# Issuing TensorE in a written order, with outer products over four row quadrants at once, in an attention and MLP backward kernel

## The chip, the cores and the metric

The kernel runs on one core of one Trainium2 chip. The metric is the device time of one execution in microseconds (us). A "round" runs both kernels on the same chip, one after the other; I quote medians. On one core a run is called slow when it is more than 1.5% above the fastest run of the same kernel in the same batch, and fast otherwise. Each run lists its mean granted TensorE clock as a share of full speed.

The parts of the core, in the profile's short names: PE is TensorE (PEld its weight loads), DVE is VectorE, ACT is ScalarE, POOL is GpSimd, SP is SyncE, which issues the loads here. POOL issues the stores. SBUF is the memory on the core, PSUM the small memory that TensorE writes to.

## The reference, cut to what matters

One decode step (one query token, batch 2) of grouped-query attention with a cache plus a bilinear MLP, and the gradients of everything for a given `grad_out`:

```python
q = (layernorm(x) @ wq)                     # 32 query heads, 16 kv heads, Dh = 128
scores = einsum("bhqd,bhkd->bhqk", q, k) * Dh ** -0.5      # 4096 positions
o = einsum("bhqk,bhkd->bhqd", softmax(scores), v)
out = x + o @ wo + ((xn @ w_gate) * (xn @ w_up)) @ w_down  # F = 4608, D = 576
_out, _vjp = jax.vjp(f, A_x, A_k_cache, A_v_cache, A_wq, A_wo, B_w_gate, B_w_up, B_w_down)
```

All inputs are read once and every gradient has the size of its input: 92.5 MB in, 92.5 MB out. With one token, the gradients of the caches and of the weights are outer products. So there is little arithmetic for each byte, but it comes as many small matmuls.

## The kernel before

The main loop has 16 steps. A step takes two K heads and two V heads of one batch entry, 1 MB each. Three kinds of TensorE work fill a step:

- **Scores.** VectorE transposes half a head, then 16 matmuls of 128 columns accumulate into one PSUM tile. The 16 come as two quarters of 8.
- **Outer products** for the gradients of K and V. 128 rows are used as four quadrants of 32, each with its own matmul (`32*128` in the profile below: 32 rows, 128 weight columns). One unit of work below does two quadrants, fills one `ps_o` buffer, and is copied out ("evicted") by ACT, or sometimes DVE, into a store tile.
- **Contractions**: 64 matmuls of 32 weight columns that reduce two heads over their positions.

```python
sb  # SBUF, by tag:  "nat" 12 buffers (loads), "st" 4 (cache-gradient stores),
    #                "sw" 2 (weight-gradient stores), "X" 3 (transposed halves)
ps  # PSUM, by tag:  "m" 2, "sc" 2 (scores), "o" 2 of [P, 2, 512] FP32
def ps_o():
    return ps.tile([P, 2, 512], FP32, tag="o", bufs=2, name="ps_o")
...
def head_scores(n, t, x, s_ps, half):
    X = xtile([P, NCH, 64], "X")
    t32(view(pairs(X...)), view(pairs(n...)))           # DVE transpose, 1.23 us
    for e in range(2):
        for c8 in range(8):
            nc.tensor.matmul(s_ps[:], lhsT=view(W[t][:], ...), rhs=view(X[:], ...), ...)
...
def outer_units(rows, bd, b, l0, oview):
    def unit(A, cp):                       # A: which pair of quadrants
        def f():
            if cp == 0:
                m["st"] = stile([P, 2, 2, 8, Dh], "so")
            o = ps_o()
            for k in range(2):
                for aa in range(2):
                    a = 2 * A + aa
                    nc.tensor.matmul(view(o[:], ...), lhsT=rows[32 * a:32 * a + 32, 2 * cp + k, :],
                                     rhs=bd[32 * a:32 * a + 32, :], start=True, stop=True)
            evac(view(m["st"][:], ...), o[:]..., 1024)
            if cp == 3:                    # two stores of 512 KB
                for aa in range(2):
                    nc.gpsimd.dma_start(oview[b, 2 * A + aa, :, l0:l0 + 2], m["st"][:, aa]...)
    return [unit(A, cp) for A in range(2) for cp in range(4)]
...
def slot(src, t, b, l, s_ps, per, mid=None):
    n = head_load(src, b, l)
    head_scores(n, t, l % 2, s_ps, 0)
    more(2)                                # two outer units
    if mid: mid()
    head_scores(n, t, l % 2, s_ps, 1)
    more(2)
    other(per)                             # MLP and group work
```

Four steps share a group of heads. At a group's end its weight gradients are staged in the two "sw" buffers: `sto` (gradient of the output weight, two tiles), then `stq` (gradient of the query weight, two tiles). The MLP's staging tiles `stw` and `std` use the same two buffers.

The order of the instructions on each engine isn't the order of this text: a scheduler reorders them when the kernel is built. Each engine then works through its own list and waits for what other engines or transfers must have done.

## Time and profile before

| | before |
|---|---|
| median time (first three runs) | 571.89 us (568.31 to 573.84) |
| span of the profiled run | 561.8 us |
| PE busy, granted clock | 472.1 us (84%), 0.802 |
| ACT, DVE busy | 343.6 us (61%), 369.6 us (66%) |
| DMA engines busy | about 87% of the span |

The prediction below shows the busy shares, the slices and six windows. What it doesn't show are the four largest TensorE groups of the page. A line gives the source line, engine, operation, output and inputs, the count; after the bar the busy time in us and the mean ns of one; after the second bar the engine's idle time just before these instructions and what ended most of it.

```profile
L503 PE MATMUL ps_sc<-X,W 128*128 128x128 bf16 x2048 | 185.8, 240 | 2.5 <-DVE X L102 2.4
...
L549 PE MATMUL ps_o<-bd,prm 32*128 32x256 bf16 x512 | 52.9, 304 | 10.5 <-ACT stq L93 4.7
L549 PE MATMUL ps_o<-bd,dsm 32*128 32x256 bf16 x512 | 54.8, 302 | 6.8 <-ACT so L93 4.4
L518 PE MATMUL ps_m<-kv,rowT 128*32 128x128 bf16 x2048 | 56.3, 251 | 1.0 <-issue 0.9
```

### The profile page before, as it was taken

The page shows a single profiled execution, that of the slowest core. Times are in us where ns is not written, and L with a number is a line of the kernel's source. Part 1 is how long each engine was busy: PE and PEld are TensorE (multiplying, and loading weights), DVE is VectorE, ACT ScalarE, POOL GpSimd, SP SyncE. Part 2 cuts the span into 40 slices and gives each one's busy share as a digit, 9 for nine tenths or more (in the row PEclk, how much of TensorE's full clock was granted, in tenths as well). Part 3 has the DMA queues.
Part 4 walks back from the last instruction along what each step waited for, and adds up shares of the span by engine and source line. Part 5 has one row for each costly group of instructions (what it writes and reads, how often), then busy time and mean ns, then how long its engine had stood idle before and what let it go on. Part 6 is the DMA issues. An engine that isn't in the chain of part 4 may idle for free. (4 is left out here: it accounts for less than half of the span.)

```text
span 561.8 us, 18035 instructions
## 1 busy us (share of the span) xinstructions
PE 472.1 (84%) x7897; PEld 336.5 (60%) x7897; DVE 369.6 (66%) x637; ACT 343.6 (61%) x473; POOL 193.3 (34%) x404
## 2 busy tenths in 40 slices
PE   2688859998989799999888973999898999888842
PEld 1576637676766465676677752666676666666511
DVE  8696836747656545738577672685787567788336
ACT  1146856857666264657667662686767559778631
POOL 5222443422432233333423441263433324433231
PEclk9899987857885655558888995697999569999656
DMA  8996999999699599689997897799999979985471
GB/s 259 407 395 225 418 407 383 339 369 365 189 412 404 199 304 410 229 305 395 360 398 270 342 418 310 263 404 415 363 399 381 420 275 385 394 347 219 158 270 49
DMA packets 53927, 186.13 MB, mean 331 GB/s; under 512 B 5164, under 2 KB 20152, under 8 KB 45656
## 3 DMA queue, kind: packets, MB, share of 16 engines
q1 hardware_dynamic: 28392, 92.49, 44.1%
q0 software_dynamic: 25456, 92.48, 42.1%
q8 instruction: 62, 1.02, 0.7%
q14 instruction: 17, 0.14, 0.1%
HBM read 92.48 MB, written 92.48 MB: 329 GB/s over the span
## 5 line engine op out<-in xcount | busy, mean ns | idle before, releaser
L93 ACT CAST so<-ps_o 128x1024 bf16<-128x1024 f32 x240 | 231.9, 1023 | 93.9 <-PE ps_o L549 90.1
L503 PE MATMUL ps_sc<-X,W 128*128 128x128 bf16 x2048 | 185.8, 240 | 2.5 <-DVE X L102 2.4
L102 DVE STREAM_TRANSPOSE X<-kv 128x1024 f32<-128x1024 f32 x128 | 157.5, 1233 | 33.6 <-PE ps_sc L503 27.7
L503 PEld LDWEIGHTS <-W 128*128 128x128 bf16 x2048 | 144.0, 107 | 34.6 <-issue 28.7
L556 POOL DMA_DIRECT2D out_dram<-so x128 | 91.4, 716 | 169.7 <-ACT so L93 74.0
L549 PE MATMUL ps_o<-bd,prm 32*128 32x256 bf16 x512 | 52.9, 304 | 10.5 <-ACT stq L93 4.7
L549 PE MATMUL ps_o<-bd,dsm 32*128 32x256 bf16 x512 | 54.8, 302 | 6.8 <-ACT so L93 4.4
L518 PE MATMUL ps_m<-kv,rowT 128*32 128x128 bf16 x2048 | 56.3, 251 | 1.0 <-issue 0.9
L518 PEld LDWEIGHTS <-rowT 128*32 128x32 bf16 x2048 | 38.4, 110 | 17.2 <-issue 13.8
L93 ACT CAST stw<-ps_o 128x1024 bf16<-128x1024 f32 x32 | 31.4, 1023 | 15.6 <-PE ps_o L364 8.8
L467 POOL COPY W<-rep 32x16 bf16<-32x16 bf16 x128 | 30.7, 240 | 20.6 <-PE ps_sc L503 13.7
L549 PEld LDWEIGHTS <-prm 32*128 32x128 bf16 x512 | 21.4, 98 | 22.6 <-issue 11.1
L549 PEld LDWEIGHTS <-dsm 32*128 32x128 bf16 x512 | 21.3, 98 | 19.8 <-issue 10.8
L93 ACT CAST std<-ps_o 128x576 bf16<-128x576 f32 x36 | 23.0, 648 | 12.9 <-PE ps_o L397 12.6
L474 POOL COPY dM<-qd 128x128 bf16<-128x128 bf16 x32 | 9.1, 289 | 61.7 <-PE ps_m L480 38.2
L93 ACT CAST stq<-ps_o 128x1024 bf16<-128x1024 f32 x10 | 9.9, 1013 | 28.3 <-DMA out_dram<-sto 26.1
L102 DVE STREAM_TRANSPOSE Xw<-wgu 128x1152 f32<-128x1152 f32 x18 | 24.5, 1362 | 3.3 <-PE ps_sc L503 3.3
L90 DVE CAST so<-ps_o 128x1024 bf16<-128x1024 f32 x16 | 19.3, 1208 | 11.1 <-PE ps_o L549 10.3
L93 ACT CAST sto<-ps_o 128x576 bf16<-128x576 f32 x30 | 18.8, 641 | 12.5 <-PE ps_o L684 12.3
L722 DVE TENSOR_SCALAR oT<-ps_m 128x4 bf16<-128x4 f32 x16 | 2.7, 170 | 35.4 <-PE ps_m L527 35.4
L371 POOL DMA_DIRECT2D out_dram<-stw x18 | 13.6, 753 | 23.0 <-ACT stw L93 11.5
L533 DVE TENSOR_TENSOR dsm<-ds,maskc 128x1024 bf16<-128x1024 bf16 x16 | 19.0, 1186 | 0.0
(178 smaller groups left out, 586.5 us busy)
## 6 DMA issues: line engine op xcount, KB each, us to landing
out_dram<-so POOLq DMA_DIRECT2D x128, 512.0 KB, 8.9
kv<-in_A_k_cache_dram SPq DMA_DIRECT2D x32, 1024.0 KB, 10.3
kv<-in_A_v_cache_dram SPq DMA_DIRECT2D x32, 1024.0 KB, 10.3
out_dram<-stw POOLq DMA_DIRECT2D x18, 512.0 KB, 9.1
wd<-in_B_w_down_dram SPq DMA_DIRECT2D x9, 576.0 KB, 9.5
out_dram<-std POOLq DMA_DIRECT2D x9, 576.0 KB, 6.9
wo<-in_A_wo_dram SPq DMA_DIRECT2D x4, 1152.0 KB, 13.6
wgu<-in_B_w_gate_dram SPq DMA_DIRECT2D x9, 512.0 KB, 11.7
```

Source lines behind the costliest of these rows:

```text
L90: nc.vector.tensor_copy(out=out, in_=in_)
L93: nc.scalar.copy(out, in_)
L102: nc.vector.transpose(out, in_)
L371: nc.gpsimd.dma_start(out[0:512, f0:f0 + FS].rearrange("(c p) n -> p c n", p=P), st[:])
L467: nc.gpsimd.tensor_copy(view(W[t][:], 32 * a, 32, 28 + 32 * a, [[2 * WW, 4], [WW + 2, 2], [1, 2]]), view(st["rep"][:], 32 * a, 32, t * 4 * ...
L474: nc.gpsimd.tensor_copy(view(dM[:], 0, P, t * 2 * P, [[P + 2, 2], [4, 32], [1, 2]]), view(st["qd"][:], 0, P, (2 if t == 0 else 1) * GH * 2 ...
L503: nc.tensor.matmul(s_ps[:], lhsT=view(W[t][:], 0, P, (be * 2 + x) * WW + 28 - 4 * c8, [[1, P]]), rhs=view(X[:], 0, P, c8 * 64 + e, [[8 * 6 ...
L518: nc.tensor.matmul(o_ps[32 * cg:32 * cg + 32, :], lhsT=view(rowsT[:], 0, P, c4 * 32 + 4 * c8, [[1, 32]]), rhs=head[:, 8 * c4 + c8, :], sta ...
L533: nc.vector.tensor_tensor(m[:], view(rows[:], 0, P, 0, [[0, 8], [1, P]]), view(maskc[:], 0, P, 0, [[1, 8], [0, P]]), ALU.mult)
L549: nc.tensor.matmul(view(o[:], 0, P, 512 * aa + P * k, [[256, 2], [1, P]]), lhsT=rows[32 * a:32 * a + 32, 2 * cp + k, :], rhs=bd[32 * a:32 ...
L556: nc.gpsimd.dma_start(oview[b, 2 * A + aa, :, l0:l0 + 2], m["st"][:, aa].rearrange("p x c d -> p x (c d)"))
L722: nc.vector.tensor_scalar(st["oT"][:, 1, 4 * s:4 * s + 4, b], t_ps[:], SCALE, None, op0=ALU.mult)
```

## The change

The intent: TensorE's instruction list is cut into very small pieces by the scheduler, and each piece costs time beyond its matmuls: in the trace of before, at full clock, scores inside a piece start 57 ns apart, and 16 of them take 1.02 us to the next piece's start, 0.11 us more than 16 x 57 ns. So TensorE alone is to issue in the order of the program text, and the text is rewritten as an even pattern of dense blocks. An outer unit now takes all four quadrants, so that four matmuls are to run side by side, and one such unit stands between the two quarters of each score block.

```diff
+    ctx.enter_context(tc.manual_schedule(engines={mybir.EngineType.PE}))
 ...
         for e in range(2):                              # head_scores
+            if e == 1:
+                yield                                   # one outer unit goes here
 ...
-        def unit(A, cp):                                # outer_units
+        def unit(cp):
             def f():
                 if cp == 0:
-                    m["st"] = stile([P, 2, 2, 8, Dh], "so")
-                o = ps_o()
+                    m["st"] = [stile([P, 2, 2, 8, Dh], "so") for _ in range(2)]
+                o = [ps_o(), ps_o()]
                 for k in range(2):
-                    for aa in range(2):
-                        a = 2 * A + aa
-                        nc.tensor.matmul(view(o[:], ...), ...)
-                evac(view(m["st"][:], ...), o[:]..., 1024)
+                    for a in range(4):
+                        nc.tensor.matmul(view(o[a // 2][:], ...), ...)
+                for A in range(2):
+                    evac(view(m["st"][A][:], ...), o[A][:]..., 1024)
                 if cp == 3:
-                    for aa in range(2):                 # two stores, twice in a block
+                    for a in range(4):                  # four stores at once
 ...
-            m["so"] = swtile([P, 4, D], "sto")          # group end: one tile, then the other
+            m["so"] = [stq([P, 4, D], "sto") for _ in range(2)]   # both at once
 ...
+        for j in range(8):                              # main loop: 8 slots in a step
+            ...
+            next(rest)                                  # first quarter
+            more()                                      # one outer unit
+            for _ in rest: pass                         # second quarter
+            if j == 0: ... prev["oV"] = contract(prev["pT"], prev["V"])
+            if j == 2: ... prev["oK"] = contract(prev["dsT"], prev["K"])
+            if 4 <= j < 7: soft[j - 4]()                # softmax in three units
+            if j == 6: outs += outer_units(cur["prm"], cur["bd1"], b, l0, ovview)
```

(All cut.) The other outer products are rewritten in the same way. The next group's weights are loaded one step earlier, `stq` and `sto` of the last group are staged in "nat" buffers, and the units of the MLP are spread over the slots. No byte of input or output and no matmul shape changes.

## The prediction

> **What bounds the kernel now.** I read the page's busy shares and slices first, then windows of 20 us, then TensorE's own timeline, then who waits for whom, and last the chain of work that ended last. The page:
>
> ```profile
> PE 472.1 (84%) x7897; PEld 336.5 (60%) x7897; DVE 369.6 (66%) x637; ACT 343.6 (61%) x473; POOL 193.3 (34%) x404
> ...
> PEclk9899987857885655558888995697999569999656
> DMA  8996999999699599689997897799999979985471
> ...
> q1 hardware_dynamic: 28392, 92.49, 44.1%
> q0 software_dynamic: 25456, 92.48, 42.1%
> ```
>
> Two resources stand out. TensorE is busy 84% at a mean granted clock of 0.80. The DMA engines have 44.1 + 42.1 + 0.8 (instruction fetch) = 87% of 561.8 us of work, or 489 us. The change moves no byte and alters no descriptor's size, so these 489 us stay. The windows tell which one bounds when (columns: span, busy of PE, PEld, DVE, ACT, POOL, then clock, DMA share, GB/s):
>
> ```profile
> 60.00:80.00 20.00, 14.83 (x276) 10.36 (x275) 13.43 (x25) 13.55 (x19) 8.36 (x15) 0.98 1.02 415
> 180.00:200.00 20.00, 16.18 (x220) 10.02 (x218) 12.44 (x18) 7.88 (x10) 6.23 (x14) 0.59 0.62 242
> 220.00:240.00 20.00, 19.28 (x268) 13.33 (x266) 12.39 (x24) 11.94 (x17) 5.30 (x12) 0.59 0.67 258
> 320.00:340.00 20.00, 13.88 (x253) 9.49 (x252) 13.22 (x23) 11.59 (x18) 7.65 (x17) 0.88 1.02 417
> 340.00:360.00 20.00, 14.28 (x200) 8.66 (x201) 11.17 (x18) 8.44 (x11) 4.52 (x8) 0.59 0.68 254
> 520.00:540.00 20.00, 14.84 (x255) 8.55 (x248) 8.42 (x14) 12.50 (x16) 5.61 (x9) 0.59 0.51 188
> ```
>
> In two of these TensorE has a clock near 0.9 or more and leaves 5 to 6 us idle, and DMA is full. In the others the clock is 0.59 and DMA starves. So the kernel is DMA-bound where TensorE is warm, and bound by TensorE (or by a wait in its queue) where it is cold. DMA's idle time, 561.8 - 489 = 73 us, is what can be won. From the windows: about 3 us at the start, 31 us after 482 us (79.8 us at share 0.61, when the last read has been issued), and so some 39 us in dips between.
>
> That the dips come through TensorE is in the sync queue's waits and in one stall:
>
> ```profile
> SPq L491 <- PE ps_m L518: 190.7, 19, 21.5
> ...
> 187.98 1.01 ACT L93 CAST stq<-ps_o 128x1024 bf16<-128x1024 f32 x1 [6.54 <-DMA out_dram<-sto]
> ...
> 189.05 0.61 PE L549 MATMUL ps_o<-bd,prm 32*128 32x256 bf16 x4 [3.83 <-ACT stq L93]
> ```
>
> Cache loads wait, 190.7 us in 19 waits, for the contraction that frees a buffer. And at 189 us TensorE waits for an eviction which itself waits for a store; afterwards the clock is about half until 255 us (0.54 over 189 to 255), though TensorE is busy 64.7 of those 66 us.
>
> [...] warm, an outer piece of 8 matmuls in two quadrants takes 0.54 us to the next start and one of 4 takes 0.32, so 4 more cost 0.22 us[...]: they run in pairs. [...] 16 score matmuls take 1.02 us to the next start[...], so about 0.12 us per change. [...]
>
> **The change part by part, in TensorE time.** I took from its timeline the time from each piece's start to the next start: score (L503) 192 us in 261 pieces, outer products (L549) 105 us in 215 pieces, contractions (L518) 65 us in 94 pieces, and the rest; about 980 pieces in 552 us, of which 76 us are waits. So TensorE's own work is 476 us.
>
> - Four quadrants. An L549 unit now takes 8 matmuls at four abreast: (8/4) x 0.107 + 0.12 = 0.33 us warm, 0.55 cold; 128 units are 42 to 70 us against 105. Saved: about 50. The other outer products (L364, L397, L654, L684, L382, L671: 61 us with waits) save about 20 in the same way.
> - Dense blocks. A contraction of 64 in one piece is 1.01 us warm and 1.83 cold; 32 of them are 32 to 59 against 65. Saved: about 15. Scores stay at 256 pieces of 8, since a unit now stands between the quarters, so they gain only through the clock.
> - Fewer pieces elsewhere (the scheduler split the MLP blocks, transposes and maxima among scores): about 100 fewer at 0.12 = 12 us.
>
> Sum: about 100 us of 476, so 376 us of work, 67% of the old span. Almost none of this is directly on the end: it turns TensorE from the bound of the cold stretches into an engine with slack, and the kernel goes to its DMA floor, 489 us plus what stays idle.
>
> What stays idle. Start: 3 us. Dips: buffers are held somewhat longer (the K contraction moves two slots on, the next group's weights are loaded a step earlier, with the same 12 buffers), and the two sw buffers at a group's end still make stq wait for sto, three times. I take 25 of the 39 us. Tail: the last group's staging gets free nat buffers (the chain has one 6.51 us wait for sto at 541.6 us, and an earlier one of 12.67 us for so), the output row is finished before the outers, and units are evicted with both engines. I take 20 of the 31 us. That is 489 + 3 + 25 + 20 = 537 for the span of an unlucky profile. Against it, warmer and evenly spaced work may fill the dips further: 10 us of them give 527. I take 530. The timed runs of before (median 571.9) lie 1.4% over the profiled one (563.6, span 561.8), so 530 + 2, times 1.014, gives about 539; [...]I put 537.
>
> **The rivals.**
> 1. *The eviction cycle becomes the bound.* A unit takes both ps_o buffers, so the next unit can't start until both are evicted. Before, 240 of 256 so evictions went to ACT at 1.02 us; two in a row are 2.05, and with 0.5 for matmuls and handover a unit costs 2.55 us with nothing double buffered. 128 such, plus 18 gate/up units at 2.55, 18 down units at 1.8, 9 tails at 1.3, and 28 back units at about 2 come to 326 + 46 + 32 + 12 + 56 = 472 us. That is close to the floor of 489 and, with the other ACT work (bd, o_sb, exp: about 30 us) partly on top, it gives 500 plus start and tail: 545 to 565 for the time. For it: PE is in order, so a unit held up holds the scores too. Against it: ACT and DVE can take one each, and scores and contractions fit in the gap.
> 2. *TensorE goes cold anyway.* With slack it waits more, and if it falls to half clock it needs about 247 us for scores alone (2048 x 0.107 + 256 x 0.12) and by the same sums some 560 in all; the time would stay at 565 to 580. [...] Against it: 60 to 80 us, with 5 us of idle, kept 0.98.
> 3. *The written order waits in the wrong places* (softmax, maskings, the bd weights from POOL): with PE in order each wait is paid. The steps between producer and use are one slot of about 3.4 us, more than the 1.2 us of a transpose or a mask, so I give this 10%: 560 to 590.
> 4. *The transfers fill completely*: nothing idle but start and tail: 489 + 3 + 15 = 507, timed 512.
>
> **Range and chances.** The middle is 537; rival 4 sets the lower end near 508, rival 1 and part of 2 the upper near 565. Faster by over 2% means under 560.5: 0.80. Within 2%: 0.15. Slower: 0.05.
>
> **What would show it.** Right: L549 has 128 pieces of 8, start to next start near 0.33 us when warm; TensorE busy under 400 us with clock over 0.85; DMA share sum still near 489 us, with fewer dips; SPq's waits for L518 shorter; the last read earlier and the tail after it under 70 us. Wrong: PE's waits for ACT so well over the present 13 us, with ACT nearly without idle (rival 1); clock under 0.7 (rival 2); PE waits for DVE or POOL of tens of us (rival 3); or a sum of DMA time that itself moves, since I assume it fixed.

Its small times can be read in the trace of the kernel before (from one start to the next, medians; the granted clock is recorded there as 1.0 or 0.5). Scores start 57 ns apart at full clock and 107 ns at half. In the outer products at full clock, 377 of 619 gaps are under 30 ns, and those of 50 to 300 ns have a median of 107 ns: two quadrants at a time, 0.107 us for 256 columns. Its 0.12 us per change is an estimate; the 16 scores above give 0.11. That trace shows only two quadrants in an outer piece, so four at once is the prediction's assumption.

## The result, and the profile after

The changed kernel takes **623.44 us** (median of four fast runs, 623.07 to 626.31) against 572.87 us (568.31 to 578.96) for the kernel before in the same rounds: ratio 1.092, with a 95% interval of 1.085 to 1.100. A ratio here is the mean time of one kernel's fast runs over the mean of the other's fast runs of the same rounds, so it isn't quite the ratio of the medians. The change is slower by 9%; the prediction said 537 us, and the result lies outside its range and outside all of its rivals.

The page of the kernel after, with the lines that answer those of before (busy time and share of each engine, clock and DMA in tenths of 40 slices, the two queues, the chain that ended last, the TensorE groups):

```profile
PE 457.4 (74%) x7897; PEld 334.5 (54%) x7897; DVE 371.9 (60%) x649; ACT 347.5 (56%) x473; POOL 187.4 (30%) x404
...
PEclk9986867587675756778775567778775667788655
DMA  8985989489697799995998689996999688975374
...
q1 hardware_dynamic: 28392, 92.49, 41.1%
q0 software_dynamic: 25456, 92.48, 40.6%
...
L510 PE MATMUL ps_sc<-X,W 128*128 128x128 bf16 x2048 | 210.1, 262 | 10.2 <-DVE X L104 10.0
...
L558 PE MATMUL ps_o<-bd,prm 32*128 32x256 bf16 x512 | 40.7, 354 | 34.9 <-DVE prm L543 23.0
L558 PE MATMUL ps_o<-bd,dsm 32*128 32x256 bf16 x512 | 39.6, 328 | 34.1 <-ACT sto L95 22.3
L525 PE MATMUL ps_m<-kv,rowT 128*32 128x128 bf16 x2048 | 49.2, 272 | 0.0
```

Read the groups first. The outer products (L549 before, L558 after) are busy for 40.7 + 39.6 = 80.3 us instead of 107.7: four quadrants side by side do save 27 us of matmul time. But the idle time in front of them has grown from 10.5 + 6.8 = 17.3 to 34.9 + 34.1 = 69.0 us, by 52 us. And the scores, whose matmuls are the same, take 210.1 us instead of 185.8, at a clock that fell from 0.802 to 0.719 (in the trace after, too, scores start 57 ns apart at full clock and 107 ns at half). PE is busy a little less (457.4 against 472.1 us) in a span that is 59.5 us longer (621.3 against 561.8), so the time with no matmul rose from 89.7 to 163.9 us.

Four of the windows that the prediction shows (span, busy us of PE, PEld, DVE, ACT, POOL with instruction counts, clock, DMA share, GB/s):

```profile
60.00:80.00 20.00, 16.50 (x285) 12.04 (x285) 8.39 (x16) 13.44 (x20) 8.43 (x18) 0.76 1.00 353
180.00:200.00 20.00, 11.13 (x207) 8.09 (x204) 6.27 (x11) 8.51 (x12) 5.22 (x12) 0.59 0.90 347
...
340.00:360.00 20.00, 16.08 (x226) 11.16 (x226) 13.26 (x21) 12.28 (x18) 5.41 (x11) 0.55 0.66 221
520.00:540.00 20.00, 16.00 (x268) 11.18 (x267) 13.20 (x22) 14.75 (x21) 5.72 (x13) 0.72 0.92 346
```

Where DMA was full before at 415 GB/s and clock 0.98 (60 to 80 us), it is still full, but at 353 GB/s. So the share of DMA time isn't a fixed quantity of work: the same bytes took 0.87 x 561.8 = 489 us before and 0.824 x 621.3 = 512 us after. From the records of the transfers (30 us after the start to 70 us before the end, smoothed over 3 us): reads and writes ran at the same time for 297 us at 395 GB/s before, and for 219 us at 366 GB/s after. Reads alone took 52 us at 304 GB/s before and 122 us at 310 after; writes alone 96 us at 281 and 145 us at 304. So the change separated the two directions.

These rates don't say that one direction alone is slow, since they include time in which the engines had little to do. Counted only over stretches of 1 us in which the engines were full (share above 0.97; a direction counts from 40 GB/s on), both directions together moved 408 GB/s before and 386 after, reads alone 354 and 381, writes alone 393 and 364; all full stretches together 397 and 378. The changed kernel is slower at both directions together too. The rates of before, weighted with the stretches of after, give 388, so by this estimate the separation accounts for about half of the fall from 397 to 378. What makes the rest isn't shown.

The waits (engine and line, what it waited for; us in total, times, the longest):

```profile
ACT so L95 <- PE ps_o L558: 125.4, 115, 6.3
...
ACT sto L95 <- DMA out_dram<-stw: 23.9, 3, 8.3
PE ps_o L558 <- DVE prm L543: 23.0, 13, 5.3
PE ps_o L558 <- ACT sto L95: 22.3, 3, 7.8
PE ps_o L558 <- ACT stw L95: 13.6, 25, 0.6
```

They name three different costs. Each can be read in TensorE's timeline (start, us, engine, line, operation, count; in brackets how long the engine was idle before it, and what ended that).

*An outer unit stands in the list before its data is ready.* Between 72 and 86 us:

```profile
80.73 1.25 DVE L104 STREAM_TRANSPOSE X<-kv 128x1024 f32<-128x1024 f32 x1 [7.50 <-DMA kv<-in_A_k_cache_dram]
...
82.13 0.33 DVE L602 TENSOR_SCALAR pr<-ex,rz 128x128 bf16<-128x128 f32 x1
82.50 1.23 DVE L543 TENSOR_TENSOR prm<-pr,maskc 128x1024 bf16<-128x1024 bf16 x1
83.78 0.61 PE L558 MATMUL ps_o<-bd,prm 32*128 32x256 bf16 x8 [5.31 <-DVE prm L543]
```

VectorE waited 7.50 us for a cache load. Behind that transpose, in VectorE's own list, stood the steps that make `prm`, which have nothing to do with that load. TensorE's next instruction needed `prm`, and so TensorE waited 5.31 us. The prediction's rival 3 had counted a slot of about 3.4 us between producer and use against 1.2 us for the mask, without the load that VectorE may be waiting for.

*A unit takes both eviction buffers*, and *a staging tile waits for a store.* Between 178 and 203 us:

```profile
182.72 1.93 ACT L95 CAST stw<-ps_o 128x1024 bf16<-128x1024 f32 x2 [0.22 <-PE ps_o L363]
...
183.79 0.29 PE L558 MATMUL ps_o<-bd,dsm 32*128 32x256 bf16 x2 [0.17 <-ACT stw L95]
...
184.70 0.39 PE L558 MATMUL ps_o<-bd,dsm 32*128 32x256 bf16 x6 [0.62 <-ACT stw L95]
...
199.39 0.64 ACT L95 CAST sto<-ps_o 128x576 bf16<-128x576 f32 x1 [8.31 <-DMA out_dram<-stw]
...
200.08 0.61 PE L558 MATMUL ps_o<-bd,dsm 32*128 32x256 bf16 x6 [7.77 <-ACT sto L95]
```

At 183 us ACT copies the two `ps_o` buffers of one unit out, 1.93 us for the pair (the 8 matmuls of the unit at 187.97 us take 0.61). The next unit wants both: it issues two matmuls when the first is free, waits 0.62 us for the second, and the scores behind it wait too. At 190.4 us ACT has begun the first `sto` tile. The second is wanted in the same unit, while its "sw" buffer still holds `stw` on its way out. ACT waits 8.31 us for that store, and TensorE, in its written order, 7.77 us for ACT. The chain that ended last (start, us, what) passes through such stores three times, and the chain of before doesn't hold them:

```profile
184.95 14.34 DMA out_dram<-stw
...
326.04 14.11 DMA out_dram<-stw
...
466.87 14.69 DMA out_dram<-stw
```

The waits for buffers of the cache loads hardly changed: with all that it waits for, the sync queue stands 319 us before the issues of cache loads, where it stood 327 (the prediction showed the largest entry of these, 190.7 us for the contraction; after, the largest are 102.5 us for a small matmul and 67.1 for the contraction). The lead of a cache load, from its issue to its first transpose, fell from 27.3 to 19.3 us (the upper of the two middle ones of 60 loads; the lower ones are 27.1 and 16.7), and 20 of 60 loads have less than 13 us, where 2 had.

### The profile page after: what moved, and what is told of

Same layout as the page of the kernel before. It is cut to its first block, busy times and chain, and to the rows that moved or that the text cites. A ratio compares the mean times of both kernels' runs of the same rounds, so it can differ in the third digit from the quotient of the medians.

```text
span 621.3 us, 18002 instructions
## 1 busy us (share of the span) xinstructions
PE 457.4 (74%) x7897; PEld 334.5 (54%) x7897; DVE 371.9 (60%) x649; ACT 347.5 (56%) x473; POOL 187.4 (30%) x404
## 3 DMA queue, kind: packets, MB, share of 16 engines
q8 instruction: 62, 1.02, 0.6%
## 4 chain that ended last, share of the span: by engine, by line
PE 31%; ACT 13%; DVE 11%; DMA 9%; issue 5%; POOL 2%; POOLq 0%; ACTq 0%; DVEq 0%
PE ps_sc L510 11%; ACT so L95 7%; DMA out_dram<-stw 7%; PE ps_o L558 7%; PE ps_m L525 5%; DVE X L104 4%; DMA out_dram<-sto 3%; ACT stw L95 2%; DVE prm L543 2%; ACT stq L95 1%; DVE so L92 1%; POOL out_dram L566 1%; PE ps_m L274 1%; PE ps_o L363 1%; PE ps_m L442 1%
## 5 line engine op out<-in xcount | busy, mean ns | idle before, releaser
L95 ACT CAST so<-ps_o 128x1024 bf16<-128x1024 f32 x239 | 231.0, 1014 | 144.1 <-PE ps_o L558 125.4
L510 PE MATMUL ps_sc<-X,W 128*128 128x128 bf16 x2048 | 210.1, 262 | 10.2 <-DVE X L104 10.0
L510 PEld LDWEIGHTS <-W 128*128 128x128 bf16 x2048 | 158.7, 116 | 61.4 <-issue 56.7
L558 PE MATMUL ps_o<-bd,prm 32*128 32x256 bf16 x512 | 40.7, 354 | 34.9 <-DVE prm L543 23.0
L558 PE MATMUL ps_o<-bd,dsm 32*128 32x256 bf16 x512 | 39.6, 328 | 34.1 <-ACT sto L95 22.3
L525 PE MATMUL ps_m<-kv,rowT 128*32 128x128 bf16 x2048 | 49.2, 272 | 0.0
L558 PEld LDWEIGHTS <-prm 32*128 32x128 bf16 x512 | 11.3, 99 | 49.7 <-DVE prm L543 26.4
L558 PEld LDWEIGHTS <-dsm 32*128 32x128 bf16 x512 | 11.7, 96 | 48.8 <-issue 44.5
L472 POOL COPY W<-rep 32x16 bf16<-32x16 bf16 x128 | 24.5, 192 | 37.4 <-PE ps_sc L510 27.1
L257 POOL COPY Wt<-Wm 64x128 bf16<-64x128 bf16 x26 | 7.5, 288 | 56.0 <-DVE Wm L251 46.8
L104 DVE STREAM_TRANSPOSE Xw<-wq 128x1152 f32<-128x1152 f32 x8 | 11.0, 1371 | 20.5 <-PE ps_sc L510 20.5
L531 ACT COPY o_sb<-ps_m 128x128 f32<-128x128 f32 x32 | 8.6, 269 | 21.9 <-PE ps_m L525 21.9
```

The costliest lines, as they stand in the source:

```text
L95: nc.scalar.copy(out, in_)
L104: nc.vector.transpose(out, in_)
L472: nc.gpsimd.tensor_copy(view(W[t][:], 32 * a, 32, 28 + 32 * a, [[2 * WW, 4], [WW + 2, 2], [1, 2]]), view(st["rep"][:], 32 * a, 32, t * 4 * ...
L510: nc.tensor.matmul(s_ps[:], lhsT=view(W[t][:], 0, P, (be * 2 + x) * WW + 28 - 4 * c8, [[1, P]]), rhs=view(X[:], 0, P, c8 * 64 + e, [[8 * 6 ...
L525: nc.tensor.matmul(o_ps[32 * cg:32 * cg + 32, :], lhsT=view(rowsT[:], 0, P, c4 * 32 + 4 * c8, [[1, 32]]), rhs=head[:, 8 * c4 + c8, :], sta ...
L531: nc.scalar.copy(o_sb[:], o_ps[:])
```

## The experiments

The theories, by the letters that the expectations use for some of them: **W**, the written order: TensorE waits for whatever stands next, and nothing can step in front. **P**, the pairing: a unit takes both `ps_o` buffers (and both store tiles), so nothing is double buffered. **R**, the reads: loads are issued later relative to their use. **C**, the clock: TensorE goes below full clock because its work is spread out. A further one, bursts: four stores at once separate the two directions of the transfers.

Kernels that start from the changed one have an `a` or `c` in front (`c` for combinations, `d` for the last), those that start from the one before a `b`. Differences to the changed kernel are taken from its 623.44 us, which was measured in another batch; the kernel before had medians of 572.9, 573.1, 571.9, 570.5, 574.9 and 570.8 us in the six batches, so batches differ by up to about 4 us. The five batches of experiments ran on five chips. Under the scheduler's order every edit also makes a new schedule, and what a new schedule alone changes wasn't measured: a few us by such a comparison aren't a finding. All results were correct.

### Is it the written order? `a_auto`

```diff
-    ctx.enter_context(tc.manual_schedule(engines={mybir.EngineType.PE}))
```

> The changed kernel with its one scheduling line taken out: TensorE's order is again chosen by the scheduler, all else stays. Theory W (the written order itself makes TensorE wait, since a late transpose or mask holds everything behind it): 570 to 590 us, and TensorE's waits fall from 153 us to under 100. Theory R (cache buffers are held longer, loads start late: median lead of a load over its first transpose 19 us against 27 before) and theory P (a unit that takes both output buffers has no double buffering): 605 to 630, since buffers and units are the same.

597.21 us (five runs, 595.97 to 609.05; the three fast ones at 595.97 to 597.21), ratio 1.045 [1.036, 1.053]. So the one line costs 623.44 - 597.21 = 26 us, half of the loss. The profile fell on a slow run; I take one wait from it further down and compare no times. The time lies between the two expectations: the other half stays under the scheduler's order, so W can't be all.

### Is it the pairing? `a_split`

Every outer unit becomes two halves of two quadrants, each with its own `ps_o`, and its own eviction right behind; the order is otherwise the same.

```diff
-                o = [ps_o(), ps_o()]
-                for k in range(2):
-                    for a in range(4):
-                        nc.tensor.matmul(view(o[a // 2][:], ...
                 for A in range(2):
+                    o = ps_o()
+                    for k in range(2):
+                        for a in (2 * A, 2 * A + 1):
+                            nc.tensor.matmul(view(o[:], ...
                     evac(...)
```

> Each outer unit is made of two halves of two quadrants again, each with its own output buffer and its own eviction right behind it; the written order and all places stay. Theory P (lost double buffering of the output buffers): 590 to 605 us and TensorE's waits for evictions (so, stw, std: some 45 us) fall under 20 us. Theories R and W: 615 to 635, a little slower even, since the quadrants run in pairs (about 0.2 us more for 128 units, 25 us of TensorE time that is partly hidden).

615.46 us, ratio 1.076 [1.062, 1.089]: 8 us better than the changed kernel. TensorE's waits for ACT (20 us for `so`, 10.6 for `stw`; 26 and 17 before this edit) shrink only a little. This is at the edge of what theories R and W gave, and far from what P gave: in the written order the handover of the two buffers isn't the largest cost.

The edit also shows something that I had overlooked. The matmuls of the K and V outer products are busy for 81.8 us here, against 80.3 with whole units, and a piece of 8 takes as little time to the next start when warm (0.336 us against 0.330). Two half units that stand next to each other in the list, on different quadrants, are as fast as one whole unit. So the saving never needed both `ps_o` buffers at once.

### Is it the reads? `a_late` and `a_early`

`a_late` loads the next group's weights one step later, as before. `a_early` puts the V contraction at slot 7 of its own step and the K contraction at slot 1 of the next, to free the buffers sooner.

```diff
-            if n % 4 == 2 and g + 1 < NGRP:                     # a_late
-                nxt, nfront = front_units(g + 1, *group_loads(g + 1))
             if new:
+                nxt, nfront = front_units(g + 1, *group_loads(g + 1))
```
```diff
-                    prev["oV"] = contract(prev["pT"], prev["V"])  # a_early: at j == 0
+                if j == 7:
+                    cur["oV"] = contract(cur["pT"], cur["V"])
```

> The next group's weights are loaded one step later, at the start of the group's last step as before the change, and its front runs in the second half of that step; this gives the cache two of the twelve buffers for one step in four. Theory R: 600 to 612 us, the median lead of loads rises from 19 to over 21 us. Theories P and W: within 1% of 623, 617 to 630.

> V is contracted in the last slot of its own step and K one slot earlier, so that four cache buffers come free one slot (about 4.5 us) sooner in every step. Theory R: 600 to 612 us, median lead of loads up by about 3 us or more. Theories P and W: within 1% of 623, or slower if the contraction now waits for the probabilities' transpose.

`a_late`: 619.42 us, ratio 1.086 [1.080, 1.091]; the median lead of a load rose from 19.3 to 22.7 us, and the time fell by 4 us. `a_early`: 626.07 us, ratio 1.097 [1.092, 1.103], no gain. Its lead didn't rise either (19.5 us), so `a_early` says little of theory R. The 4 us of `a_late` are no more than batches differ by, and the two intervals overlap (1.085 to 1.100 for the changed kernel): a gain from 3 us more of lead is possible, not shown.

### The pairing in the old order: `b_quad`

The kernel before, with all outer units made four-quadrant units as in the change (both `ps_o`, both store tiles, four stores at once), and nothing else. The edit is the `outer_units` part of the diff above, the same for the other outer products, and:

```diff
-        more(2)
+        more(1)
```

> The kernel before, with scheduler and order of the program as they were, but every outer unit made of four quadrants over both output buffers, with both store tiles filled together and stored together, as the change has it. Theory Q (the four-quadrant unit is itself a loss: no double buffering of outputs, both staging tiles taken at once, stores in bursts of 2 MB): 588 to 605 us, near the changed kernel under the scheduler (597), with more time in which only one direction of DMA runs (148 us before). Theory S (the loss lies in the new places of the work: later contractions, earlier weights, softmax spread over slots): 560 to 578.

593.41 us (four runs, 592.41 to 598.18). The kernel before had 559.59 to 579.03 in seven runs, median 571.9. The two sets of runs don't overlap, and by the medians the four-quadrant units cost 21.5 us in the old order. That is what is left over: in the path from before over `b_quad` and `a_auto` to the changed kernel, 21.5 us for the four-quadrant units and 26 for the written order come to 48 of the 51 us between the medians. Put differently, the change without its written order (597 us) is level with the kernel before plus four-quadrant units (593 us). All else that the change moved comes to about 4 us, no more than batches differ by.

The waits of `b_quad` show where its time goes (PE busy 485.0 us and clock 0.756, against 472.1 and 0.802):

```profile
ACT stq L93 <- DMA out_dram<-sto: 33.7, 5, 11.5
...
ACT stw L93 <- DMA out_dram<-std: 21.1, 5, 10.2
...
DVE stw L90 <- DMA out_dram<-std: 14.3, 2, 7.3
```

All three are waits of an evicting engine for a staging tile that is still being stored. Before, the first was 26.1 us and the other two 6.3 and 2.6. The saving hardly appears: the K and V outer products are busy for 103.1 us against 107.7, since the scheduler cuts the units again (226 pieces, 45 of them of all 8 matmuls).

### The single waits: `a_oseq`, `a_prm`

`a_oseq` finishes one `sto` tile after the other, so that the second is wanted later; the unit still has four matmuls, two quadrants of both halves. `a_prm` queues the V outer products one slot later.

```diff
-        def outer_o(h2, k):                                     # a_oseq
-                    m["so"] = [stq([P, 4, D], "sto") for _ in range(2)]
+        def outer_o(A, h2):
+                    m["so"] = stq([P, 4, D], "sto")
```
```diff
                 if j == 6:                                      # a_prm
                     cur["bd0"] = build_bd(st, b, s, 0)
+                if j == 7:
                     outs += outer_units(cur["prm"], cur["bd1"], b, l0, ovview)
```

> The changed kernel with one unit type undone: the products for the output weights' gradient fill one staging tile after the other (two quadrants in a matmul group, both output buffers), instead of both at once; nothing else moves. Theory G (at a group's end the sto units need both staging tiles at once and wait until both gate/up stores have landed; 14 us on the chain three times): 590 to 608 us, and TensorE's wait for sto falls from 23 us to under 10. Otherwise: 617 to 628.

> The changed kernel with the V outer products one slot later, so that the masked probabilities have one more slot to be ready. Theory W (the written order waits for late VectorE results): TensorE's wait for prm falls from 23 us to under 8 and the time to 600 to 612. If that wait only stands in for the late cache load that holds VectorE: it turns up as a wait for X or so instead and the time stays at 617 to 630.

`a_oseq`: 602.22 us (601.18 to 603.52), 21 us better. The waits of `sto` for `out_dram<-stw` are gone, and the one for `prm` is as before:

```profile
PE ps_o L558 <- DVE prm L543: 23.4, 13, 6.3
...
ACT stq L95 <- DMA out_dram<-sto: 0.9, 1, 0.9
```

`a_prm`: 603.6 us (601.84 to 607.23), 20 us better. The `prm` wait is nearly gone, and a wait for staging has come up in another place:

```profile
PE ps_o L558 <- DVE prm L543: 4.9, 4, 1.5
...
ACT stq L95 <- DMA out_dram<-sto: 21.7, 4, 8.5
```

`a_oseq` is the clean case: TensorE's waits fall by 27 us in all (from 143 to 115), and the time by 21. The stores of `stw`, 43 us of the chain that ended last before the edit, are gone from it. This is the most direct evidence that in the written order such a wait lies on the path. `a_prm` is less clean. With the wait for `prm` (-18 us) the one for `sto` fell too (from 23.5 to 8.3), the one for `stq` rose (from 12 to 27), and TensorE's waits fell by only 7 us in all, from 143 to 135; its busy time fell by 15 us (457.4 to 442.7) at a higher clock (0.748 against 0.719). So the edit is worth 20 us, but not simply as the wait that it was made for.

### Do bursts of stores matter? `a_amaj`, later `b_burst`

`a_amaj` takes `a_split` and fills the first store tile before the second, so that stores leave as 1 MB every two slots.

```diff
-        return [unit(cp) for cp in range(4)]
+        return [unit(A, c2) for A in range(2) for c2 in range(2)]
```

> The changed kernel as in the split run (615 us), and the K/V outer products fill the first store tile in two slots and then the second, as before, so that 1 MB is stored every two slots rather than 2 MB every four. Theory B (bursts of stores keep reads and writes apart: 219 us with both directions at 366 GB/s, against 297 us at 395 before): 590 to 605 us, both directions together for over 250 us. Otherwise within 1% of the split run: 609 to 622.

634.76 us, 19 us worse than `a_split`. Reads and writes did run together for longer, 290 us instead of 219 for the changed kernel, though at 365 GB/s, and yet it was slower. This expectation missed: in the written order, bringing the directions together brought no gain. It isn't a clean test, though: two half units in a row now use the same two quadrants, and the K and V outer products are busy for 112.2 us instead of 81.8.

`b_burst`, run later, tries the same on the kernel before: half units as they were, each with its own `ps_o`, but both store tiles filled side by side and 2 MB stored at once.

```diff
-        def unit(A, cp):
-                    m["st"] = stile([P, 2, 2, 8, Dh], "so")
+        def unit(cp):
+                    m["st"] = [stile([P, 2, 2, 8, Dh], "so") for _ in range(2)]
+                for A in range(2):                       # half units, one ps_o each
```

> The kernel before, with only the K/V outer products reordered: both store tiles are filled side by side, half units with their own output buffers as before, and stored together, 2 MB at once. Theory B (bursts): 582 to 595, as the four-quadrant version in the old order (593), and DMA in both directions falls from 297 us to under 250. Theory P (pairing the output and sw buffers): 566 to 578, no change.

580.38 us, ratio 1.013 [1.006, 1.020]: 7 us by the ratio. By the same count of directions, both together fell to 226 us, about as in the changed kernel. So the bursts are about a third of what `b_quad` costs. The remaining 14 us are then left to the paired `ps_o` buffers and to the staging of the weight gradients; these two I didn't separate.

### Is it the clock? `a_fill`, `b_fill`, `c_three_fill`

Two useless matmuls of 128 x 128 x 512 in front of each K or V unit (256 in all), into PSUM that the unit overwrites. They add 256 x 512 columns, which is 55 us at full clock by an estimate from the trace of before (0.107 us for 256 columns there, so 0.214 us for 512).

```diff
                 for k in range(2):
+                    nc.tensor.matmul(o[0][:, k, :], lhsT=ident[:], rhs=dyr[:, 0:512], start=True, stop=True)
+                for k in range(2):
                     for a in range(4):
```

`b_fill` does the same in the kernel before, one for each of its 256 half units.

> The changed kernel with two useless 128x128 matmuls of 512 columns before each of the 128 K/V outer units, into the output buffer that the unit then overwrites: work added, nothing else. In the nine traces so far the clock of a window of 3.4 us is full after a window in which the matmuls' cells (columns x rows/128 x weight columns/128, in cycles at full clock) were in use for more than 0.37 of the time, and half after one with less; the mean is 0.342 in the changed kernel and 0.380 before. The fillers add 131 thousand cycles, or 55 us at full clock, 0.09 of the span. Theory C (cold TensorE is a main cause of the loss): the granted clock rises from 0.72 to over 0.85 and the time falls to 590 to 612 although work is added. Theory L (local waits and late loads set the time, the clock only follows): the clock rises, the time stays at 618 or rises to 650.

> The kernel before with one such filler before each of its 256 half units (the same 131 thousand cycles). Theory C: clock from 0.80 to over 0.9, time 550 to 568 against 572, as cold stretches such as 190 to 255 us vanish. Theory L: 572 to 590, the fillers cost more than they bring.

The share that the first expectation speaks of is a fit to the traces, not shown to be the mechanism. Their clock records come in steps of 3.413 us and hold full or half clock alone. In the traces of both kernels (331 steps with a next one), a threshold of 0.375 on the share in one step (a matmul's columns x rows/128 x weight columns/128, at 0.107 us for 256 columns) misjudges the clock of the next step in 16 cases; the best threshold on the time that PE is busy misjudges 92. Over ten traces (both kernels and the first eight runs, 1,709 steps) it was 77 against 540, and in `a_fill` and `b_fill`, which the fit hadn't seen, 29 of 348. The mean share was 0.380 before and 0.342 after; a matmul on 32 rows counts a quarter in it. So PE can be busy and its clock low: 64.7 of 66 us after the stall at 189 us of the kernel before, at 0.54.

`a_fill`: 643.55 us, ratio 1.126 [1.116, 1.137]: 20 us worse.

```profile
span 642.5 us, 18444 instructions
...
PE 460.2 (72%) x8074; PEld 316.1 (49%) x8153; DVE 371.3 (58%) x649; ACT 346.4 (54%) x473; POOL 187.5 (29%) x404
```

The clock rose from 0.719 to 0.842, and the time at half clock fell from 349 to 203 us. PE's busy time is about what it was (460 against 457 us; 79 of 8,153 matmul records are missing): the warmer clock paid for the 55 us of useless work. But the time without a matmul rose from 163.9 to 182.3 us and the kernel got slower. `b_fill`: 600.6 us (588.15 to 605.21; only one of its runs counts as fast), about 30 us worse by the medians, 18 by the fast runs alone. So a clock warmed in this way doesn't bring the time back in either kernel. Theory C isn't refuted by it. The fillers stand on TensorE's way: if all of their 55 us lie on the path, a warm clock that costs nothing would be worth 55 - 20 = 35 us, and less if fewer of them do (an estimate). The clock fell with the change; how much of the loss goes through it stays open.

### The repairs together: `c_three`, `c_three_fill`, `c_split`, `c_three_auto`

`c_three` has the edits of `a_late`, `a_oseq` and `a_prm`. `c_three_fill` adds the two useless matmuls, `c_split` halves all units as `a_split` does, and `c_three_auto` takes out the written order.

```diff
-    ctx.enter_context(tc.manual_schedule(engines={mybir.EngineType.PE}))   # c_three_auto, on c_three
```

> The changed kernel with three of the tried edits together: the output-weight products one staging tile after the other (alone -21 us), the V products one slot later (alone -20), the next group's weights a step later (alone -4). If the losses are separate waits they add up: 573 to 585 us, level with the kernel before. If one makes room that another wait takes up: 590 to 603.

> The same with the fillers. Theory C: below the version without fillers by 10 us or more, perhaps below the kernel before: 550 to 575. Theory L: 0 to 20 us above the version without fillers.

> The three-edit version with all outer units as two halves, each with its own output buffer, as in the split run (alone -8 us). Theory P: 575 to 582. If the handover has become slack: 586 to 594.

> The three-edit version (588 us) without the written order. If the written order costs by itself, apart from the two mended waits: 565 to 580. If the two waits were all that it cost: 584 to 596; a gain of the written order in what is left: 598 or more.

`c_three`: 588.35 us (580.41 to 593.45), ratio 1.027 [1.015, 1.038]. The single gains were 4 + 21 + 20 = 45 us; together they are 35, so they add up in good part. PE is busy 437.9 us of 585.8.

`c_three_fill`: 603.0 us, ratio 1.048 [1.034, 1.063]: the filler costs again, 15 us.

`c_split`: 582.25 us, ratio 1.014 [1.007, 1.021]: halving the units again gives about 6 us by the medians, but the two intervals overlap, so it isn't told apart from nothing.

`c_three_auto`: 569.94 us, ratio 0.994 [0.987, 1.001]: 18 us better than `c_three`, level with the kernel before. So even with its worst waits repaired, the written order costs 18 us here. In this kernel VectorE waits 62 us for cache loads, and still the time is level with before. So late loads (theory R) need not make the kernel slower than before; whether it would be faster without them isn't shown.

### A version that beats both: `b_natq`, `b_natall`, `d_new_natq`

The kernel before has the same staging trouble at a group's end, only smaller:

```profile
ACT stq L93 <- DMA out_dram<-sto: 26.1, 4, 9.9
...
DVE stq L90 <- DMA out_dram<-sto: 15.8, 3, 7.4
```

`b_natq` is the kernel before with one word changed: `stq` is staged in one of the 12 "nat" buffers. `b_natall` does it for `sto` as well, and `d_new_natq` is `c_split` under the scheduler's order with the same word changed.

```diff
-                    m["st"] = swtile([P, 2, GH * P], "stq")
+                    m["st"] = nat([P, 2, GH * P], "stq")
```

> The kernel before with the query-weight staging (stq) taken from the cache's twelve buffers instead of the two sw buffers. Before, ACT and VectorE waited 42 us for sto stores there, TensorE 21 us behind them, and a cold stretch of 60 us followed one such wait. If that wait is on the path: 550 to 564 us, faster than both kernels, and TensorE's wait for stq is near 0. If the two buffers are missed by the loads instead: 570 to 585.

> The kernel before with both stq and sto staged in the cache's buffers, so that the two sw buffers serve only the MLP. If the remaining waits at sw (stw for std, 19 us; std for stw 4 us) matter: 548 to 557. If the loads miss the buffers: 560 to 575.

> The three-edit version under the scheduler (570 us) with double-buffered half units (worth 6 to 8 us in the written order) and with stq staged in a cache buffer (worth 16 us before; its wait is 17 us here). If these add: 545 to 555, below the 558 of the old places. If late loads set the pace of the new places (VectorE waits 62 us for cache loads there, 0 before): 560 to 575, for a staged stq takes one more of the twelve buffers.

`b_natq`: **558.27 us** (550.77 to 567.27), ratio 0.970 [0.961, 0.980]: faster than both kernels. The two `stq` waits are gone, and waits for the other staging tile come up, but smaller:

```profile
ACT stw L93 <- DMA out_dram<-std: 13.2, 3, 9.2
...
DVE stw L90 <- DMA out_dram<-std: 6.2, 1, 6.2
```

The price is 4 x 2 more tiles through the buffers of the loads: the median lead of a cache load goes from 27.3 to 25.4 us. `b_natall` pays more of it (22.5 us) and is at 563.52 us, ratio 0.986 [0.975, 0.998], so it isn't better than `b_natq`. `d_new_natq` is at 557.22 us, ratio 0.980 [0.970, 0.990], in another batch: not told apart from `b_natq`. With the scheduler's order, halved units and the repairs, what is left of the change neither costs nor gains within these intervals.

What couldn't be tried: more buffers. SBUF is full; a thirteenth "nat" buffer or a third "sw" buffer doesn't fit (the build asks for 194.1 and 189.6 KB a partition in the changed kernel, and has 185.19).

## Why the prediction was wrong

**The step that failed** is this one: "Almost none of this is directly on the end: it turns TensorE from the bound of the cold stretches into an engine with slack, and the kernel goes to its DMA floor", together with its "Sum: about 100 us of 476". Neither the work saved nor the slack came about: TensorE's work fell by 17 us and its waits rose by 74.

*The sum.* I took TensorE's timeline again, piece by piece, with the wait in front of the next piece taken off (which gives 484 us of work before; the 476 of the prediction had also taken off the wait before the first piece).

| TensorE work, us | before | after | change | predicted |
|---|---|---|---|---|
| K and V outer products | 96.0 | 71.9 | -24 | -50 |
| contractions | 52.5 | 46.4 | -6 | -15 |
| scores | 171.7 | 187.7 | +16 | through the clock only |
| all else | 163.4 | 160.5 | -3 | -32 |
| sum | 484 | 466 | -17 | about -100 |
| waits | 69 | 143 | +74 | fewer |

There are two errors in the terms. The prediction's 105 and 65 us (start of a piece to the next start) contain 9 and 12 us of waits, which denser pieces don't save. And its durations were a mean of warm and cold, at a clock that it expected to rise. The durations themselves were right: a whole outer unit takes 0.330 us to the next start when warm and 0.547 when cold (predicted 0.33 and 0.55), a contraction 0.96 and 1.83 (1.01 and 1.83). But the 128 units together come to 71.9 us, the cold end of the predicted 42 to 70; they stand in 156 pieces, 100 of them whole. The clock fell, and the same scores took 16 us more.

*The slack.* Waits rose by 74 us, work fell by 17, and the start was 2 us later: that is the 59 us of the span. In order of size, the waits by what ended them: ACT `so` 26 us (13 before), ACT `sto` 23.5 (3), `prm` 23 (2), ACT `stw` 17 (5), ACT `stq` 12 (21). The prediction asked for slack and forgot that TensorE, issuing in a fixed order, would turn other engines' lateness into its own idle time: 143 us of waits. With the scheduler's order before, it was 69 us.

**Step by step:**

- *The four-quadrant unit is faster by itself*: right where the unit stays whole. Its matmuls' busy time fell from 107.7 to 80.3 us. In the scheduler's order, which cuts it, it is 103.1 (`b_quad`); and two half units next to each other do as well (81.8, `a_split`).
- *DMA's 489 us stay*: wrong. 512 us, since with full engines the bytes moved at 378 GB/s instead of 397. The separated directions are by estimate about half of that, and bursts cost about 7 us in the old order (`b_burst`). In the written order their share isn't isolated (`a_amaj`).
- *Dips fill up*: wrong. DMA's idle time rose from 73 to 109 us, and that between 12 us and the last read from some 39 to some 72, where the prediction asked for 25.
- *The tail*: wrong by the prediction's own measure. From the last reads to the end it takes 80 us at a DMA share of 0.57, so 34 us of it are idle (31 before, 20 predicted). From the last transpose of a cache head to the end it is 48.5 us (51 before), so the loss of time lies in the body.
- *Rival 1, eviction*: the mechanism was there, in another form. It was argued as an ACT at its limit; ACT is busy only 347.5 us (56%) and itself waits 125.4 us for TensorE. What shows is the handover, two engines waiting for each other in turn, not the capacity of either. In the old order the whole four-quadrant form costs 21.5 us (`b_quad`); in the written order halving the units gives 8 back (`a_split`).
- *Rival 2, cold anyway*: right that it goes cold (0.719), after waits: in the trace after, the clock is full when waits of 4.91, 3.00 and 2.94 us begin (they end at 110.3, 218.9 and 276.8 us) and half when they end. `a_fill` made it warm again and slower, but with 55 us of work added, so what the cold costs stays open. (The rival's 2048 x 0.107 + 256 x 0.12 is 250 us, not 247; 0.107 us is the gap between two scores at half clock in the trace. And the half clock that the prediction dates from the stall at 189 us had ruled since 164.7 us, but for one window of 3.4 us.)
- *Rival 3, waits in the wrong places*: the prediction gave this 10%, and it is half of the loss: 26 us (`a_auto`). Its wait for `prm` was of the kind named, and moving it gained 20 us. The wait for `sto` (21 us) was in no rival: a unit that fills both staging tiles waits for two stores. It is still there without the written order (25 us in the profile of `a_auto`, a slow run), so it isn't the order alone that makes it.

**The signs that the prediction named.** TensorE busy under 400 us at a clock over 0.85: 457 at 0.72, wrong. PE's waits for ACT well over 13 us: yes, 26 for `so` alone, but not with an ACT nearly without idle time. A tail under 70 us after the last read: 80, wrong. PE's waits for DVE of tens of us: yes, 23 for `prm`. A DMA sum that moves: yes. It listed the right signs and weighed them wrongly.

**What stays open**: how the 14 us of `b_quad` beyond the bursts divide between the paired `ps_o` buffers and the staging tiles (a hint: `c_three_auto` keeps the paired `ps_o` and the bursts, fills the `sto` tiles one after the other, and is level with before); what a warm clock would be worth that costs nothing; why the DMA engines, when full, move less than before; and what more SBUF would do.

## What to carry to other kernels

Before you freeze an engine's order, list for each instruction what it waits for at that place, including what the producing engine may itself be waiting for; every such lateness becomes idle time of the frozen engine (143 us of TensorE's waits here, where it had been 69). A unit of work that takes all buffers of a kind (PSUM, store tiles, staging) gives up double buffering, and its faster matmuls may only lengthen the wait in front of it (27 us of matmul time saved here, 52 us more of idle time in front). Before you pay for that, see whether smaller units next to each other do as well (81.8 against 80.3 us here). Count a saving on an engine only after the waits in front of it are checked. And look at staging tiles where a stage ends: one word about where a tile is staged gained 3% here, more than the whole rewrite.
